# Reordering loads, stores and the first attention units in a fused attention and mixture-of-depths kernel

## The chip, the cores and the metric

The kernel runs on one core of one Trainium2 chip. The metric is the device time of one execution in microseconds; a smaller number is better. A core has five engines, each with its own stream of instructions in program order: TensorE (PE, matrix products and transposes; its weight loads are listed apart as PEld), VectorE (DVE), ScalarE (ACT), GpSimd (POOL) and SyncE (SP), which here only issues transfers. [...] In this kernel the schedule is written by hand: the order of the lines in the source is the order of each engine's instructions.

## The reference

Eight batches, eight heads, 576 positions, head dimension 64. Attention without a product of queries and keys: q is softmaxed over its head dimension, k over the positions, and `k^T v` (64 x 64 per head) is formed first. Then, for each batch, the 128 positions with the highest gate score go through an MLP (512 to 1024 to 512) and the others are passed through.

```python
def _attn_ref(q, k, v):
    q_s = np.exp(q - np.max(q, axis=-1, keepdims=True))
    q_s = q_s / (np.sum(q_s, axis=-1, keepdims=True) + 1e-09)
    k_s = np.exp(k - np.max(k, axis=2, keepdims=True))
    k_s = k_s / (np.sum(k_s, axis=2, keepdims=True) + 1e-09)
    kv = np.einsum('bhsd,bhse->bhde', k_s, v)
    return np.einsum('bhsd,bhde->bhse', q_s, kv)

def _moe_ref(x, w_gate, w1, w2, capacity):          # x: (8, 576, 512), the heads side by side
    scores = np.einsum('bsd,d->bs', x, w_gate)
    out = x.copy()
    for b in range(B):
        top_idx = np.argpartition(-scores[b], capacity)[:capacity]      # capacity 128
        xe = x[b, top_idx]
        ye = np.maximum(xe @ w1, 0.0) @ w2
        g = 1.0 / (1.0 + np.exp(-scores[b, top_idx]))
        out[b, top_idx] = x[b, top_idx] + g[:, None] * ye
    return out
```

## The kernel before

The work is cut into 16 units; a unit is four heads of one batch, so two units make one batch ("block"). All arithmetic is in fp32 but for the finding of indices. The steps of a unit u:

```python
LD = 3                                   # raw k, v, q: three buffers each, unit u uses u % 3
def load(u, which, queues=(nc.sync, nc.sync)):      # two transfers for each of k, v, q, issued by SyncE
    ...
def k_exp(u):   nc.scalar.activation(out=ke, in_=raw["k"][u % LD], func=AF.Exp)             # L217
def q_exp(u, i): nc.scalar.activation(out=st["qe", u][:, i], in_=qr[:, i], func=AF.Exp)     # L224, half i of q
def v_copy(u, engine=nc.vector):                                                           # L227
    engine.tensor_copy(out=v_ones[u % 2][:, :, :, :D], in_=raw["v"][u % LD])
def kv_mm(u):                            # L237: exp(k)^T [v, 1], 20 products
    ...
def kv_out(u):                           # DVE reciprocal L246, product with the gate weights wg L249,
    ...                                  # ACT copy to kv_w L250, DVE sum L251
def q_t(u, i, on_vector=False, wide=False):          # transposes of qe (L265 or L272), then scaled to qT
    ...                                              # on ACT (L278) or DVE (L276)
def x_mm(u, i, wide=False):              # L288 or L293: qT times kv_w, into PSUM tile "x" (two buffers)
    ...
def x_sums(u, i):   ...                  # DVE: 1 / sum (L309), gate scores (L310)
def x_scale(u, i):  ...                  # DVE: x times 1 / sum into xs (L315); xs has three buffers, one per block
def x_store(u):                          # L325: two transfers from xs to out, issued by SyncE
    ...
def kv_and_exp(u):
    kv_mm(u); q_exp(u, 0); kv_out(u); q_exp(u, 1)
def ready(u, engine=nc.vector):
    k_exp(u); v_copy(u, engine)
```

For a block b, `score` and `score_row` turn the gate scores into a row on all partitions (TensorE transposes L351, ScalarE copies L354 and L356), `compare` counts for each position how many others come before it (L364, five steps on VectorE), `hits` marks the chosen ones (L381), `find` collects their row numbers (TensorE L391), `fetch` gathers the rows back from `out` by an indirect transfer (L405, GpSimd), `turn` transposes them (L440), `mlp1` and `mlp2` are the two products of the MLP (L459, L469, eight pieces each), `finish` adds (L482) and `put` scatters the rows back (L474). Block 0 alone gets its rows by products with a one-hot matrix (`select`, L420) instead of a gather.

Units 0 to 2 are written out ahead of the loop, of which the parts touched are:

```python
    set_not_before(range(2))
    nc.vector.tensor_copy(out=wg..., in_=g_ps[:, :4 * D])
    ready(0)
    kv_mm(0)
    q_exp(0, 0)
    kv_out(0)
    q_exp(0, 1)
    load(3, "kvq")
    load_w2(0)
    ...                                   # units 0 and 1, load(4, "kvq"), load_w2(1), unit 2 up to its transposes
    for r in range(R):                    # R = 5
        compare(0, r)
        if r == N2 - 1:                   # N2 = 4
            x_mm(2, 0)
        for n in range(n_sl):             # n_sl = 1
            select(0, n, r)
    x_mm(2, 1)
    k_exp(3)
    x_out(2, 0)
    x_out(2, 1)
    v_copy(3)
    x_store(2)
```

The loop runs over s from 3 to 18. Stage s does the products of unit s (for s below 16) and half of the MLP of block (s - 3) // 2: `mlp1` in an odd stage, `mlp2` in an even one. The MLP's pieces are put between the other work to keep TensorE busy.

```python
    LAG = 3
    OWN = 3, 5, 7
    for s in range(LAG, NU + LAG):        # NU = 16
        ...
        own = s in OWN
        kv_next = s + 1 < NU and not own and s + 1 not in OWN
        ends = s // 2 if here and s % 2 == 1 else None              # the block that ends here
        chosen = (s - 2) // 2 if s % 2 == 0 and s <= NU else None   # the block whose rows are found here
        if own:
            if s > LAG:
                ready(s)
            pieces(2)
            kv_and_exp(s)
        if s == 6:
            load(8, "kvq")
        if s == 8:
            load(11, "kvq")
        if s == NU:
            each(fetch, 0)
        if here:
            q_t(s, 0)
            q_t(s, 1)
        if chosen is not None:
            each(hits, chosen)
        if kv_next:
            ready(s + 1)
        pieces(1) if own else pieces(2)
        if chosen is not None:
            each(find, chosen)
            each(fetch, chosen)
        if here:
            ...                           # x_mm, x_sums, (score), x_scale of unit s
            x_store(s)
        if s == 5:
            x_store(0)
            x_store(1)
        if kv_next:
            kv_and_exp(s + 1)
        if s < 6:
            load(s + 2, "kvq")
        elif s == 7:
            load(9, "kvq")
            load(10, "kvq")
        elif 8 <= s < NU - 4:
            load(s + 4, "kvq")
        pieces(1 if own or ends is None else 2)
        if own:
            v_copy(s + 1)
        if ends is not None:
            score_row(ends)
            if own:
                k_exp(s + 1)
            for r in range(R):
                compare(ends, r)
        if s == LAG + 1:
            for step in (hits, find, gate):
                each(step, 0)
        ...                               # gate of the chosen block
        pieces(1 if own else 3 if ends is None else 2)
        if own:
            kv_and_exp(s + 1)
        pieces(1)
        if second and mlp_b + 1 < B:
            each(turn, mlp_b + 1)
        pieces(KF - f_next)               # KF = 8
        ...                               # finish
```

In stages 3, 5 and 7 ("own") a unit's kv product is made in its own stage and the next unit's at the end of the same stage. In all other stages the kv product of the next unit is made after the x products.

Of the kernel before, what the change touches and what calls it, by code (L numbers as in the profile page):

```python
# [17 lines left out]
def kernel(  # L18
# [25 lines left out]
    N2 = R - 1  # L44
# [3 lines left out]
    KF = F // P  # L48
# [42 lines left out]
    NU = len(units)  # L91
# [116 lines left out]
    def set_not_before(rows):  # L208
        for r in rows:
            nc.vector.tensor_scalar(not_before[:, r], order_minus_p, float(r * P), TINY, op0=OP.is_ge, op1=OP.mult)  # L210
# [9 lines left out]
    def q_exp(u, i):  # L220
        if i == 0:
            st["qe", u] = at.tile([P, 2, R, 2, D], F32, tag="qe", name="qe")
        qr = raw["q"][u % LD].rearrange("p (i h) r d -> p i r h d", i=2)
        nc.scalar.activation(out=st["qe", u][:, i], in_=qr[:, i], func=AF.Exp)  # L224
# [16 lines left out]
    def kv_out(u):  # L241


        qd = units[u][1]
        kv = st.pop(("kv", u))
        nc.vector.reciprocal(out=krec[:, u], in_=kv[:, :, D])  # L246
        kw = kv_w[u % 2]
        prod = at.tile([P, 2, D], F32, tag="prod", name="prod")
        nc.vector.tensor_mul(prod, kv[:, :, :D], wg[:, qd])  # L249
        nc.scalar.copy(out=kw[:, :, :D + 1], in_=kv)  # L250
        nc.vector.reduce_sum(out=kw[:, :, D + 1], in_=prod, axis=AX.X)  # L251
# [3 lines left out]
    def q_t(u, i, on_vector=False, wide=False):  # L255

        if i == 0:
            st["qT", u] = at.tile([P, 2, R, 2, D], F32, tag="qT", name="qT")
        qe = st["qe", u] if i == 0 else st.pop(("qe", u))
        t_ps = ps.tile([P, 2, 512], F32, tag="x", name="x", bufs=2)  # L260
        if wide:
            to = st["qT", u][:, i].rearrange("p r a c -> p (r a c)")
            src = t_ps.rearrange("p a c -> p (a c)")[:, :R * P]
            for r in range(R):
                nc.tensor.transpose(out=src[:, r * P:(r + 1) * P], in_=qe[:, i, r].rearrange("p h d -> p (h d)"),  # L265
                                    identity=ident)
        else:
            to = st["qT", u][:, i].rearrange("p r a c -> p a r c")
            src = t_ps[:, :, :R * 64].rearrange("p a (r c) -> p a r c", r=R)
            for r in range(R):  # L270
                for a in range(2):
                    nc.tensor.transpose(out=t_ps[:, a, r * 64:(r + 1) * 64],  # L272
                                        in_=qe[part(a), i, r].rearrange("p h d -> p (h d)"),
                                        identity=ident[part(a), part(a)])
        if on_vector:
            nc.vector.tensor_scalar(to, src, krec[:, u, i:i + 1], None, op0=OP.mult)  # L276
        else:
            nc.scalar.activation(out=to, in_=src, func=AF.Copy, scale=krec[:, u, i:i + 1])  # L278
# [312 lines left out]
    def ready(u, engine=nc.vector):  # L591
        k_exp(u)
        v_copy(u, engine)
# [10 lines left out]
    for h in range(2):  # L604
        nc.tensor.matmul(out=g_ps[part(h), :4 * D], lhsT=ones_f,
                         rhs=w_row.rearrange("o (x h d) -> o h x d", h=2, d=D)[:, h], start=True, stop=True)
    set_not_before(range(2))
    nc.vector.tensor_copy(out=wg.rearrange("p a i d -> p (a i d)"), in_=g_ps[:, :4 * D])
    ready(0)
    kv_mm(0)  # L610
    q_exp(0, 0)
    kv_out(0)
    q_exp(0, 1)
    load(3, "kvq")
    load_w2(0)

# [32 lines left out]
    q_t(2, 0, wide=True)  # L649
    fill(4)  # L650
    q_t(2, 1, wide=True)
    for r in range(R):
        compare(0, r)
        if r == N2 - 1:
            x_mm(2, 0)
        for n in range(n_sl):
            select(0, n, r)
    x_mm(2, 1)
    k_exp(3)
    x_out(2, 0)  # L660
    x_out(2, 1)
    v_copy(3)
    x_store(2)

    LAG = 3
    OWN = 3, 5, 7
    number = good = None
    for s in range(LAG, NU + LAG):

        mlp_b, second = divmod(s - LAG, 2)  # L670
        piece = mlp2 if second else mlp1
        f_next = 0

        def pieces(n):
            nonlocal f_next
            for _ in range(n):
                each(piece, mlp_b, f_next)
                f_next += 1

        here = s < NU  # L680
        own = s in OWN
        kv_next = s + 1 < NU and not own and s + 1 not in OWN
        ends = s // 2 if here and s % 2 == 1 else None
        chosen = (s - 2) // 2 if s % 2 == 0 and s <= NU else None
        if own:
            if s > LAG:
                ready(s)
            pieces(2)
            kv_and_exp(s)
        if s == 6:  # L690
            load(8, "kvq")
        if s == 8:
            load(11, "kvq")
        if s == NU:
            each(fetch, 0)
        if here:
# [3 lines that stand above are left out]
            each(hits, chosen)  # L700
        if kv_next:
            ready(s + 1)
        if own:
            pieces(1)
        else:
            pieces(2)
        if chosen is not None:
            each(find, chosen)
            each(fetch, chosen)
        if here:  # L710
            x_mm(s, 0)
            x_mm(s, 1)
            x_sums(s, 0)
            x_sums(s, 1)
            if ends is not None:
                score(ends)
            x_scale(s, 0)
            x_scale(s, 1)
            x_store(s)
        if s == 5:  # L720
            x_store(0)
            x_store(1)
        if kv_next:
            kv_and_exp(s + 1)
        if s < 6:
            load(s + 2, "kvq")
        elif s == 7:
            load(9, "kvq")
            load(10, "kvq")
        elif 8 <= s < NU - 4:  # L730
            load(s + 4, "kvq")
        pieces(1 if own or ends is None else 2)
        if own:
            v_copy(s + 1)
        if ends is not None:
            score_row(ends)
            if own:
                k_exp(s + 1)
            for r in range(R):
                compare(ends, r)  # L740
        if s == LAG + 1:
            for step in (hits, find, gate):
                each(step, 0)
        if chosen is not None:
            each(gate, chosen)
        if good is not None and number is None:
            number = count_good(good)
        pieces(1 if own else 3 if ends is None else 2)
        if own:
            kv_and_exp(s + 1)  # L750
        pieces(1)
        if second and mlp_b + 1 < B:
            each(turn, mlp_b + 1)
        pieces(KF - f_next)
        if second:
            each(finish if mlp_b else finish_gated, mlp_b)
        if s == NU + 1:
            each(finish_rows, 0)
        if s == NU:
            good = in_range()  # L760
# [28 lines left out]
```

## Time and profile before

| | |
|---|---|
| time, median of 3 | 228.05 us (227.99 to 228.05) |
| span of the profiled execution | 228.4 us |
| transferred | 46.67 MB, mean 204 GB/s |
| busy: TensorE, VectorE, ScalarE, GpSimd | 204.3, 117.7, 86.6, 36.8 us |
| start of the loop (first MLP product) | 31.17 us |
| starts of s = 4, 5, 6, 7, 8, 9 | 46.87, 61.88, 77.49, 90.13, 105.59, 118.08 us |

The last two rows are read from the chain of work that ended last: the loop starts with the first group at L459, a later stage with the transposes of its unit (L272) or, where its kv product is its own, with the MLP pieces ahead of them. In the timelines a line holds start, length, engine, source line, operation, result and operands, shape and count, and in brackets how long the engine stood idle just before and what released it. The records count each fp32 product twice: unit products that the program issues 20 times are listed as x40.

### The profile page before, as it was taken

Reading aid. Unit: us, or ns where it says so; the run is one execution under the profiler, and the core shown is the slowest. Engines: PE = TensorE matmul, PEld = TensorE weight load, DVE = VectorE, ACT = ScalarE, POOL = GpSimd, SP = SyncE. Lnnn points to the kernel's source line nnn. Section 1 sums busy time; section 2 is a strip of 40 time slices with the busy share of each in tenths; the row PEclk is TensorE's granted clock in tenths of the full one; section 3 lists DMA queues with packets and bytes.
Section 4 is the critical chain, followed back from the end, with each engine's and each line's share of the span. In section 5 each row is a group of like instructions: output and inputs, shape, how many; then the busy total and the mean of one; then the engine's idle time right before and its main releaser. Section 6 shows DMA issues by size and latency. Waiting matters only on the chain.

```text
span 228.4 us, 7006 instructions
## 1 busy us (share of the span) xinstructions
PE 204.3 (89%) x2983; PEld 154.0 (67%) x2983; DVE 117.7 (52%) x353; ACT 86.6 (38%) x145; POOL 36.8 (16%) x93
## 2 busy tenths in 40 slices
PE   6789998896988988889999999999999999989970
PEld 2478797762577754777659965996599659747720
DVE  6477953937018651186635782568256824815010
ACT  3265444540275403455335452544354532201100
POOL 5024000311003010230113010401040103214101
PEclk9999999998899999999999999999999999999998
DMA  5999999573901999229999959468313131331101
GB/s 192 360 357 384 364 368 354 182 261 125 306 32 54 295 317 372 97 82 283 326 370 384 373 197 301 161 210 250 108 53 103 41 113 49 106 92 46 53 4 50
DMA packets 39305, 46.67 MB, mean 204 GB/s; under 512 B 2401, under 2 KB 36193, under 8 KB 39266
## 3 DMA queue, kind: packets, MB, share of 16 engines
q1 hardware_dynamic: 37712, 41.62, 54.5%
q0 software_dynamic: 1280, 4.20, 5.3%
q8 instruction: 25, 0.41, 0.7%
q10 hardware_dynamic: 274, 0.33, 0.4%
q14 instruction: 14, 0.11, 0.1%
HBM read 34.61 MB, written 11.53 MB: 202 GB/s over the span
## 4 chain that ended last, share of the span: by engine, by line
PE 64%; DVE 15%; DMA 9%; ACT 5%; issue 3%; POOL 1%; SPq 1%; POOLq 0%; ACTq 0%; DVEq 0%
PE mm L469 18%; PE mm L459 17%; PE x L293 9%; PE tp L237 8%; DVE junk L364 7%; DMA xr<-out_dram,idx 5%; PE x L272 4%; DMA q<-in_q_dram 4%; ACT qe L224 3%; DVE xs L315 3%; PE mm L420 2%; PE mm L440 1%; PE x L265 1%; PE x L288 1%; PE tp L351 1%
## 5 line engine op out<-in xcount | busy, mean ns | idle before, releaser
L459 PE MATMUL mm<-xT,w 128*128 128x128 f32 x512 | 64.2, 279 | 0.0
L459 PEld LDWEIGHTS mm<-xT,w 128*128 128x128 f32 x512 | 59.4, 192 | 3.7 <-ACT xT L447 1.9
L469 PE MATMUL mm<-w,hT 128*128 128x512 f32 x128 | 61.8, 618 | 0.0
L469 PEld LDWEIGHTS mm<-w,hT 128*128 128x128 f32 x128 | 23.0, 195 | 21.5 <-issue 20.7
L364 DVE SCALAR_TENSOR_TENSOR junk<-srow,s,not_before 128x576 bf16<-128x576 f32 x40 | 32.7, 817 | 7.8 <-ACT srow L356 6.8
L237 PE MATMUL tp<-v_ones,ke 128*64 128x65 f32 x640 | 23.3, 224 | 5.4 <-ACT ke L217 3.0
L237 PEld LDWEIGHTS tp<-v_ones,ke 128*64 128x64 f32 x640 | 20.7, 137 | 8.0 <-ACT ke L217 3.9
L224 ACT ACTIVATE qe<-q 128x640 f32<-128x640 f32 x32 | 23.5, 738 | 4.3 <-DMA q<-in_q_dram 2.5
L315 DVE TENSOR_TENSOR xs<-x,qrec 128x640 f32<-128x640 f32 x32 | 25.0, 816 | 0.0
L278 ACT ACTIVATE qT<-x,krec 128x640 f32<-128x640 f32 x30 | 22.5, 793 | 3.6 <-PE x L272 3.4
L293 PE MATMUL x<-kv_w,qT 64*64 64x66 f32 x1200 | 22.6, 221 | 1.1 <-issue 0.9
L482 DVE SCALAR_TENSOR_TENSOR o<-mm,g,xr 128x512 f32<-128x512 f32 x7 | 5.3, 751 | 34.6 <-PE mm L469 34.6
L293 PEld LDWEIGHTS x<-kv_w,qT 64*64 64x64 f32 x1200 | 19.8, 133 | 3.3 <-issue 1.6
L309 DVE RECIPROCAL qrec<-x 128x10 f32<-128x10 f32 x32 | 7.0, 220 | 28.4 <-PE x L293 28.2
L462 ACT ACTIVATE hT<-mm 128x512 f32<-128x512 f32 x16 | 9.5, 594 | 31.5 <-PE mm L459 31.5
L217 ACT ACTIVATE ke<-k 128x1280 f32<-128x1280 f32 x16 | 20.4, 1272 | 0.9 <-DMA k<-in_k_dram 0.9
L250 ACT COPY kv_w<-tp 128x130 f32<-128x130 f32 x16 | 4.3, 268 | 39.0 <-DVE prod L249 33.2
L405 POOL DMA_INDIRECT xr<-out_dram,idx x8 | 8.4, 1046 | 59.9 <-DVE sr L310 18.1
L447 ACT COPY xT<-mm 128x512 f32<-128x512 f32 x8 | 4.7, 585 | 34.2 <-PE mm L440 29.2
L474 POOL DMA_INDIRECT out_dram<-o,idx x7 | 8.3, 1182 | 55.1 <-DVE o L482 55.1
L272 PE MATMUL x<-ident,qe 64*128 64x64 f32 x260 | 12.2, 230 | 3.6 <-ACT qe L224 3.6
L272 PEld LDWEIGHTS x<-ident,qe 64*128 64x128 f32 x260 | 9.6, 139 | 8.4 <-ACT qe L224 4.4
(99 smaller groups left out, 146.6 us busy)
## 6 DMA issues: line engine op xcount, KB each, us to landing
v<-in_v_dram SPq DMA_DIRECT2D x16, 320.0 KB
q<-in_q_dram SPq DMA_DIRECT2D x16, 320.0 KB
out_dram<-xs SPq DMA_DIRECT2D x16, 320.0 KB
k<-in_k_dram SPq DMA_DIRECT2D x15, 320.0 KB
k<-in_k_dram SPq DMA_DIRECT2D x16, 256.0 KB
v<-in_v_dram SPq DMA_DIRECT2D x16, 256.0 KB
q<-in_q_dram SPq DMA_DIRECT2D x16, 256.0 KB
out_dram<-xs SPq DMA_DIRECT2D x16, 256.0 KB
```

The source lines that it names most:

```text
L217: nc.scalar.activation(out=ke, in_=raw["k"][u % LD], func=AF.Exp)
L224: nc.scalar.activation(out=st["qe", u][:, i], in_=qr[:, i], func=AF.Exp)
L237: nc.tensor.matmul(out=kv[part(h), i], lhsT=ke[:, 2 * i + h, r], rhs=vo[:, 2 * i + h, r], start=(r == 0), stop=(r == N2))
L272: nc.tensor.transpose(out=t_ps[:, a, r * 64:(r + 1) * 64], in_=qe[part(a), i, r].rearrange("p h d -> p (h d)"), identity=ident[part(a), pa ...
L278: nc.scalar.activation(out=to, in_=src, func=AF.Copy, scale=krec[:, u, i:i + 1])
L293: nc.tensor.matmul(out=x[part(c), h, r * C:(r + 1) * C], lhsT=qT[part(h), i, r, c], rhs=kv_w[u % 2][part(h), i], start=True, stop=True)
L315: nc.vector.tensor_mul(xs[b][:, :, qd, i].rearrange("p r h d -> p h r d"), x[:, :, :, :D], rec.to_broadcast([P, 2, R, D]))
L364: nc.vector.scalar_tensor_tensor(junk, st["srow", b], st["s", b][:, r:r + 1], not_before[:, r], op0=OP.subtract, op1=OP.is_ge, accum_out=s ...
L405: nc.gpsimd.indirect_dma_start(out=xr[:m], out_offset=None, in_=out_rows[:(place(b) + 1) * S], in_offset=bass.IndirectOffsetOnAxis(ap=st[" ...
L459: nc.tensor.matmul(out=h_ps[:, f % 4 * m:(f % 4 + 1) * m], lhsT=w1[:, d, f * P:(f + 1) * P], rhs=xT[:, d, :m], start=(d == 0), stop=(d == ...
L462: nc.scalar.activation(out=hT[:, f - 3:f + 1, :m], in_=h_ps[:, :4 * m].rearrange("p (f c) -> p f c", f=4), func=AF.Relu)
L469: nc.tensor.matmul(out=st["y", b, n][:m], lhsT=st["hT", b, n][:, f, :m], rhs=w2[:, f], start=(f == 0), stop=(f == KF - 1))
```

## The change

Only the order of instructions is changed. It has four parts.

- Unit 0: v's copy goes ahead of the copy of wg on VectorE, and both exps of q ahead of kv_out, which has a copy on ScalarE.
- Unit 3: its exps, v's copy and its kv product move from stage 3 to the stretch ahead of the loop. The first x product of unit 2 moves two rows earlier. With this, unit 4's kv product comes in the usual place of stage 3, after unit 3's x products.
- Of the stages with a kv product of their own only s = 5 remains, and both exps of q go ahead of that product. Unit 6's exp and copy move forward accordingly, and unit 7 is treated as any later one.
- Loads: k and v of unit 5 are issued before the loop and so before the store of unit 3; after stage s the load is always that of unit s + 3; in stage 5 unit 8's load goes ahead of the late stores of units 0 and 1.

In stage 4 the steps of block 0 (hits, find, gate), which serve only to scatter its rows later, are spread over the stage. The next block's rows are turned always one piece before the last of the MLP.

```diff
     set_not_before(range(2))
+    ready(0)
     nc.vector.tensor_copy(out=wg..., in_=g_ps[:, :4 * D])
-    ready(0)
     kv_mm(0)
     q_exp(0, 0)
+    q_exp(0, 1)
     kv_out(0)
-    q_exp(0, 1)
     ...
     q_t(2, 1, wide=True)
+    k_exp(3)
     for r in range(R):
         compare(0, r)
-        if r == N2 - 1:
+        if r == 1:
             x_mm(2, 0)
         for n in range(n_sl):
             select(0, n, r)
     x_mm(2, 1)
-    k_exp(3)
+    q_exp(3, 0)
+    q_exp(3, 1)
+    v_copy(3)
     x_out(2, 0)
+    kv_mm(3)
     x_out(2, 1)
-    v_copy(3)
+    kv_out(3)
     x_store(2)
+    load(5, "kv")
     ...
-    OWN = 3, 5, 7
+    OWN = 5
     ...
-        kv_next = s + 1 < NU and not own and s + 1 not in OWN
+        kv_next = s + 1 < NU and s + 1 != OWN
+        first_hits = s == LAG + 1
-        if own:
-            if s > LAG:
-                ready(s)
+        if s == LAG:
             pieces(2)
-            kv_and_exp(s)
-        if s == 6:
-            load(8, "kvq")
-        if s == 8:
-            load(11, "kvq")
+        if s == OWN:
+            ready(s)
+            q_exp(s, 0)
+            q_exp(s, 1)
+            pieces(2)
+            kv_mm(s)
+            kv_out(s)
     ...                                  # q_t of unit s, hits of the chosen block, ready(s + 1) if kv_next
-        if own:
-            pieces(1)
-        else:
-            pieces(2)
+        if first_hits:
+            each(hits, 0)
+        pieces(1 if s in (LAG, OWN) else 2)
     ...                                  # find, fetch; x_mm, x_sums, x_scale, x_store of unit s
-        if s == 5:
+        if s == LAG:
+            load(5, "q")
+            load(6, "kvq")
+        elif s < NU - 3:
+            load(s + 3, "kvq")
+        if s == OWN:
             x_store(0)
             x_store(1)
         if kv_next:
             kv_and_exp(s + 1)
-        if s < 6:
-            load(s + 2, "kvq")
-        elif s == 7:
-            load(9, "kvq")
-            load(10, "kvq")
-        elif 8 <= s < NU - 4:
-            load(s + 4, "kvq")
-        pieces(1 if own or ends is None else 2)
-        if own:
-            v_copy(s + 1)
+        if first_hits:
+            each(find, 0)
+        pieces(1 if ends is None else 2)
         if ends is not None:
             score_row(ends)
-            if own:
-                k_exp(s + 1)
             for r in range(R):
                 compare(ends, r)
-        if s == LAG + 1:
-            for step in (hits, find, gate):
-                each(step, 0)
+        if first_hits:
+            each(gate, 0)
     ...                                  # gate of the chosen block
-        pieces(1 if own else 3 if ends is None else 2)
-        if own:
-            kv_and_exp(s + 1)
-        pieces(1)
+        pieces(KF - 1 - f_next)
         if second and mlp_b + 1 < B:
             each(turn, mlp_b + 1)
-        pieces(KF - f_next)
+        pieces(1)
```

## The prediction

> **What bounds the kernel now.** I read the page's slices first, then a table of stages, then the TensorE timeline. The page's rows (each digit a fortieth of the span, 5.71 us):
>
> ```profile
> PE 204.3 (89%) x2983; PEld 154.0 (67%) x2983; DVE 117.7 (52%) x353; ACT 86.6 (38%) x145; POOL 36.8 (16%) x93
> ...
> PE   6789998896988988889999999999999999989970
> ...
> PEclk9999999998899999999999999999999999999998
> DMA  5999999573901999229999959468313131331101
> ```
>
> TensorE is the bound: 89% busy, no other engine over 52%, and a 64% share of the chain. From about slice 20 on it is full; in slices 5 to 19 it has gaps, and in slices 10 and 11 its clock dips. The DMA is full in slices 2 to 7 (354 to 384 GB/s), so an early gain can also run into arrivals.
>
> Next, the stages of the main loop (columns: window, length, busy and count of PE, PEld, DVE, ACT, POOL, clock, DMA share, GB/s). The first six rows are s = 3 to 8, the last two are s = 11 and 12, two undisturbed stages of the same kinds:
>
> ```profile
> 31.17:46.87 15.70, 13.57 (x257) 12.57 (x251) 10.31 (x29) 7.29 (x13) 1.80 (x7) 1.00 0.86 290
> 46.87:61.88 15.01, 12.68 (x131) 6.50 (x131) 5.72 (x19) 3.39 (x8) 1.19 (x1) 0.89 0.68 215
> 61.88:77.49 15.61, 13.54 (x252) 12.50 (x251) 8.45 (x25) 8.01 (x14) 1.79 (x7) 1.00 0.34 114
> 77.49:90.13 12.64, 10.80 (x127) 5.81 (x126) 3.67 (x12) 3.39 (x8) 1.01 (x1) 1.00 1.02 332
> 90.13:105.59 15.46, 13.46 (x250) 12.50 (x249) 9.93 (x27) 7.24 (x13) 3.13 (x8) 1.00 0.45 145
> 105.59:118.08 12.49, 11.88 (x166) 7.02 (x165) 4.96 (x17) 6.00 (x11) 1.02 (x1) 1.00 1.01 335
> 141.45:152.94 11.49, 11.49 (x211) 11.05 (x213) 7.15 (x19) 5.25 (x9) 2.65 (x8) 1.00 0.57 185
> 152.94:164.54 11.60, 11.47 (x168) 6.84 (x169) 6.45 (x20) 5.37 (x9) 1.03 (x1) 1.00 0.66 211
> ```
>
> The reader is to see that the last two rows hold almost no TensorE idle time, while s = 3, 5 and 7 take 15.5 to 15.7 us instead of 11.49. One kv product of that, 1.32 us, is extra work (those stages hold two); the rest, nearly 3 us each, is waiting. What is waited for stands in the brackets of the TensorE timeline (start, length, operation, count, idle before it and releaser):
>
> ```profile
> 9.56 1.39 PE L237 MATMUL tp<-v_ones,ke 128*64 128x65 f32 x40 [1.36 <-ACT qe L224]
> ...
> 36.19 0.53 PE L272 MATMUL x<-ident,qe 64*128 64x64 f32 x10 [1.00 <-ACT qe L224]
> ...
> 42.67 1.39 PE L237 MATMUL tp<-v_ones,ke 128*64 128x65 f32 x40 [1.01 <-ACT ke L217]
> ...
> 55.23 0.28 PE L391 MATMUL tp<-vals,hit 128*128 128x5 bf16 x5 [1.66 <-DVE hit L381]
> ```
>
> The second and third recur with 0.99 to 1.01 us at 66.82 and 73.29 (s = 5) and at 94.92 and 101.40 (s = 7).
>
> [...] around the 1.66 us wait at 55.23 its busy time is 0.77 of 2 us in 54 to 56, and the granted clock is 0.86, 0.50 and 0.79 in 54:56, 56:58 and 58:60. [...] the trace shows qe's second half at 66.03, behind kv_w's copy (65.86), which waited for VectorE. [...] SyncE's waits here show stores on DVE's xs for 46.4 us in total. [...] The gather of s = 6 took 7.30 us beside loads, the one at 201.66 took 3.27.
>
> **The change part by part.** No TensorE work is added or removed; only waits can go or come.
>
> Start. v's copy goes ahead of wg's, which waits for the small product that ends at 8.21 (7.51 + 0.70). The copy (0.82, now 8.60 to 9.42) can end by about 8.3, and the kv product starts there instead of at 9.56: 1.25 us. Both exps of q now stand ahead of kv_w's copy, so qT(0, 0) starts near 10.4 instead of 12.23. What follows soon meets arrivals: v's second unit was waited for until 12.20 on GpSimd, then the copy takes 1.25, so kv product 1 cannot start before 13.5 (now 15.90); unit 2's cannot before 17.25 + 1.25 = 18.5 (now 20.45). I take 1.9 us saved at the row's comparison and hence at the loop's start.
>
> Unit 3 ahead of the MLP. Its kv product adds 1.33 before the loop and leaves s = 3. From the GB/s row, k, v and q of unit 3 land near 25.5, 27 and 29 us; the product needs them at about 29.7, so I put no wait there. The loop starts at 31.17 - 1.9 + 1.33 = 30.6.
>
> Stages 3 to 8, from the undisturbed 11.49 (odd) and 11.60 (even):
> - s = 3: one kv product, no inner waits, the MLP in one more burst: 11.49 + 0.2 = 11.7 (was 15.70).
> - s = 4: no kv product: 11.60 - 1.33 = 10.3; find of block 0 adds 0.3. One MLP piece (about 1 us) fewer stands between the score row and find, and in the undisturbed stage hits end at 132.1, just as find is reached: 0.9 wait. Small issue gaps 0.3. The gather of block 1 falls among the loads of units 5, 6 and 7; with 7.3 us instead of 3.3 it lands up to 1.9 us after TensorE wants it: 1.2. Sum 13.0 (was 15.01). The 1.66 wait and the half clock (0.14 x 2 + 0.50 x 2 + 0.21 x 2 = 1.7 us lost) go, because block 0's hits are made next to block 1's and its find follows the x product.
> - s = 5, still its own: two kv products, 11.49 + 1.33; exps of q before the product end near the product's end (k's exp 1.27, two exps about 1.4), so only 0.2 for one more burst and 0.2 for k's exp of unit 6: 13.2 (was 15.61).
> - s = 6: 11.60 + 0.9 (find again, one piece fewer) + 0.3 = 12.8; it now holds unit 7's kv product (was 12.64 without).
> - s = 7: 11.5 (was 15.46). s = 8: 11.60 + 0.3 = 11.9 (was 12.49).
>
> Sum: 11.7 + 13.0 + 13.2 + 12.8 + 11.5 + 11.9 = 74.1, so s = 9 starts at 30.6 + 74.1 = 104.7 instead of 118.08. The order from s = 9 on is the same but for loads three units ahead instead of four. A load issued after s's store still has over 1.5 stages, about 17 us, until its k is used, and three arrays of 0.59 MB at 370 GB/s take 4.8. So the rest stays 228.40 - 118.08 = 110.3: span 215.0, and 214.7 by the median, which is 0.35 under the profiled span. My list takes each wait that I found and none that I didn't; I add 1.3 for those: **216.0 us**.
>
> **Rivals.**
> 1. Arrivals take the gain. For it: DMA is full to about 40 us, and unit 4's k, v, q land near 33, 35 and 36.5 while the new order asks for them from 34.5 on; v's copy stands in VectorE's FIFO ahead of unit 3's sums, so a late v holds the x buffers. Against it: in my schedule these miss by under 0.6 us. If each early arrival costs, the start's 1.9 us and another 1.5 go: about 219.5.
> 2. The gather becomes the wait. Loads that used to sit behind stores run early, so block 1's gather shares the engines with up to three units' loads. For it: 7.30 against 3.27 us. If it lands 3 us late, TensorE may also fall to half clock as at 55 us: 3 + 1.7 less the 1.2 counted, so 219.5.
> 3. The stores of units 0 and 1 now go behind unit 8's load. They free the buffer that s = 6's xs writes; by my count they land near 74 us, where VectorE wants it at 72.5. That holds VectorE 1.5 us beside 7 us of TensorE work, so nothing; if the backlog is 8 us longer it costs about 2 to 3 us.
> 4. Everything fits and no arrival shows: without the 1.3 and the 1.2, 213.5.
>
> **Range and chances.** The waits removed are read from the trace, 12 to 13 us with the start, and none of the rivals gives back more than 4 alone. Two together reach 222. So 212.8 to 220.5, faster by over 2% (under 223.5) 0.93, within 2% 0.05, slower 0.02.
>
> **What would show it.** Right: the first kv product near 8.3; the loop's first MLP product near 30.6; no bracket from qe or ke of about 1 us in s = 3, 5, 7; clock 1.00 throughout 45 to 60; s = 9 starting near 105; a small bracket from hit before find in s = 4 and 6; the tail as long as before. Wrong: TensorE idle from DMA (v, k or xr) of over 2 us, a dip of the clock in the loop, VectorE waiting for out_dram stores near s = 6, or the loads of s over 9 arriving late.

## The result and the profile after

The changed kernel took 216.76 us (median of 4, 215.09 to 218.49) against 228.05 us: a ratio of 0.948, 95% interval 0.9426 to 0.9535. The ratios here and below are of the mean times of undisturbed executions (the record counts the 218.49 as disturbed, in a state of lower clock, 0.985 instead of 0.994 to 0.995), the medians of all. The profiled execution spans 214.7 us instead of 228.4; as a whole that execution took 216.52 us, and the profiled one of the kernel before 230.25, which is 2.2 over its median. Differences between the two traces are therefore larger than those between the times: 13.7 us of span against 11.3. The page's rows for it:

```profile
PE 197.9 (92%) x2980; PEld 151.2 (70%) x2983; DVE 118.9 (55%) x353; ACT 87.4 (41%) x145; POOL 35.4 (16%) x93
...
PE   5998998889999899999979999999999999899970
...
PEclk9999999999999999999999999999999999999997
DMA  5999999997937999494949387586930412311101
```

TensorE's busy time fell by 6.4 us, though it does the same work: 1.7 us of that is, by the prediction's estimate, the half clock that is gone from slices 10 and 11 (before, the granted clock was 0.50 from 55.45 to 58.86; now it is 1.00 in all six stages below). Of the rest a part lies in the x products (L293): one takes 221 ns in both kernels, but the time covered by all 1200 records fell from 22.6 to 21.2 us, so they overlap more. The other 7.3 us are idle time. The DMA is now full up to slice 9 instead of 7.

The stages, s = 3 to 8 and the rest (columns as before: window, length, busy and count of PE, PEld, DVE, ACT and POOL, clock, DMA share, GB/s):

```profile
31.46:45.05 13.59, 12.00 (x215) 11.29 (x211) 6.37 (x20) 5.92 (x11) 1.33 (x7) 1.00 1.07 376
45.05:55.76 10.71, 10.13 (x132) 5.59 (x131) 7.84 (x25) 2.89 (x6) 1.19 (x1) 1.00 0.91 303
55.76:69.15 13.39, 13.12 (x252) 12.35 (x253) 6.27 (x19) 8.65 (x14) 1.33 (x7) 1.00 0.63 196
69.15:81.11 11.96, 11.38 (x167) 6.66 (x169) 7.33 (x22) 5.38 (x9) 1.02 (x1) 1.00 0.99 323
81.11:93.11 12.00, 11.77 (x212) 11.19 (x213) 7.18 (x19) 5.38 (x9) 2.66 (x8) 1.00 0.73 239
93.11:104.38 11.27, 11.27 (x167) 6.79 (x169) 6.43 (x20) 5.37 (x9) 1.03 (x1) 1.00 0.71 222
104.38:214.70 110.32, 100.73 (x1397) 76.58 (x1397) 53.58 (x154) 37.30 (x64) 19.64 (x41) 0.99 0.45 144
```

The six stages take 72.9 us instead of 86.9, 1.33 of which moved ahead of the loop; the rest of the program takes 110.3 as before. The idle times on TensorE that remain (start, length, operation, count, idle before and releaser):

```profile
8.28 1.39 PE L237 MATMUL tp<-v_ones,ke 128*64 128x65 f32 x40 [0.17 <-DVE v_ones L227]
...
37.28 0.65 PE L237 MATMUL tp<-v_ones,ke 128*64 128x65 f32 x15 [0.58 <-DVE qrec L309]
38.94 0.92 PE L237 MATMUL tp<-v_ones,ke 128*64 128x65 f32 x25 [1.01 <-issue]
...
48.33 0.28 PE L391 MATMUL tp<-vals,hit 128*128 128x5 bf16 x5 [0.58 <-DVE hit L381]
...
62.55 1.39 PE L237 MATMUL tp<-v_ones,ke 128*64 128x65 f32 x40 [0.19 <-ACT ke L217]
...
72.40 0.28 PE L391 MATMUL tp<-vals,hit 128*128 128x5 bf16 x5 [0.57 <-DVE hit L381]
...
111.19 2.05 PE L459 MATMUL mm<-xT,w 128*128 128x128 f32 x16 [1.42 <-issue]
```

The brackets of about 1 us from qe and ke are gone. Two kinds are new. One is a wait at 37.28 for VectorE's copy of unit 4's v:

```profile
36.31 0.83 DVE L227 COPY v_ones<-v 128x1280 f32<-128x1280 f32 x1 [4.04 <-DMA v<-in_v_dram]
```

The copy ended at 37.14 and the product starts 0.14 us later, as unit 0's does after its copy; the bracket names the reciprocal that VectorE did next, which the product does not read. The other kind are gaps put down to "issue", in the middle of a product or ahead of one, of which more below.

### The profile page after: what moved, and what is told of

Its sections match the earlier page's. It is cut to its first block, busy times and chain, and to the rows that moved or that the text cites. A ratio compares the mean times of both kernels' runs of the same rounds, so it can differ in the third digit from the quotient of the medians.

```text
span 214.7 us, 7006 instructions
## 1 busy us (share of the span) xinstructions
PE 197.9 (92%) x2980; PEld 151.2 (70%) x2983; DVE 118.9 (55%) x353; ACT 87.4 (41%) x145; POOL 35.4 (16%) x93
## 4 chain that ended last, share of the span: by engine, by line
PE 64%; DMA 14%; DVE 12%; ACT 3%; issue 3%; POOL 1%; POOLq 0%; ACTq 0%; DVEq 0%
PE mm L469 22%; PE mm L459 20%; DMA v<-in_v_dram 8%; PE x L293 7%; PE tp L237 7%; DVE junk L364 6%; DMA q<-in_q_dram 4%; PE x L272 3%; DMA xr<-out_dram,idx 2%; PE mm L440 2%; PE tp L351 1%; DVE hit L381 1%; DVE not_before L210 1%; ACT srow L354 1%; ACT qT L278 1%
## 5 line engine op out<-in xcount | busy, mean ns | idle before, releaser
L459 PE MATMUL mm<-xT,w 128*128 128x128 f32 x512 | 63.0, 278 | 1.4 <-issue 1.4
L469 PE MATMUL mm<-w,hT 128*128 128x512 f32 x128 | 59.9, 603 | 0.0
L469 PEld LDWEIGHTS mm<-w,hT 128*128 128x128 f32 x128 | 22.6, 190 | 20.8 <-issue 19.9
L237 PE MATMUL tp<-v_ones,ke 128*64 128x65 f32 x640 | 22.7, 224 | 2.9 <-issue 1.2
L237 PEld LDWEIGHTS tp<-v_ones,ke 128*64 128x64 f32 x640 | 20.2, 137 | 4.9 <-issue 2.1
L293 PE MATMUL x<-kv_w,qT 64*64 64x66 f32 x1200 | 21.2, 221 | 0.1
L293 PEld LDWEIGHTS x<-kv_w,qT 64*64 64x64 f32 x1200 | 19.0, 134 | 1.8 <-ACT qT L278 0.6
L227 DVE COPY v_ones<-v 128x1280 f32<-128x1280 f32 x14 | 11.5, 821 | 5.6 <-DMA v<-in_v_dram 5.6
L272 PEld LDWEIGHTS x<-ident,qe 64*128 64x128 f32 x260 | 9.1, 139 | 4.7 <-ACT xT L447 3.8
```

The source lines that it names most:

```text
L237: nc.tensor.matmul(out=kv[part(h), i], lhsT=ke[:, 2 * i + h, r], rhs=vo[:, 2 * i + h, r], start=(r == 0), stop=(r == N2))
L272: nc.tensor.transpose(out=t_ps[:, a, r * 64:(r + 1) * 64], in_=qe[part(a), i, r].rearrange("p h d -> p (h d)"), identity=ident[part(a), pa ...
L293: nc.tensor.matmul(out=x[part(c), h, r * C:(r + 1) * C], lhsT=qT[part(h), i, r, c], rhs=kv_w[u % 2][part(h), i], start=True, stop=True)
L459: nc.tensor.matmul(out=h_ps[:, f % 4 * m:(f % 4 + 1) * m], lhsT=w1[:, d, f * P:(f + 1) * P], rhs=xT[:, d, :m], start=(d == 0), stop=(d == ...
L469: nc.tensor.matmul(out=st["y", b, n][:m], lhsT=st["hT", b, n][:, f, :m], rhs=w2[:, f], start=(f == 0), stop=(f == KF - 1))
```

## The experiments

The kernel before took 228.0 to 230.7 us on the chips that were used, so each version is judged by its ratio to the kernel before on its own chip; 0.01 is 2.3 us. Some versions ran on one chip and can also be set against each other: the new start, all but the move, the old start and the old steps; both versions of the loads, the 72 instructions, and w2 late; the changed kernel once more and the two versions with the MLP ahead. "Old" below means the order of the kernel before.

| version | median us | ratio and interval |
|---|---|---|
| before, new start only | 226.86 | 0.9937 (0.9901 to 0.9972) |
| before, new loads only | 229.18 | 0.9937 (0.9911 to 0.9963) |
| before, all but the move of the units | 221.74 | 0.9763 (0.9644 to 0.9882) |
| changed | 216.76 | 0.948 (0.9426 to 0.9535) |
| changed, once more | 219.26 | 0.9537 (0.9487 to 0.9587) |
| changed, old start | 216.75 | 0.9533 (0.9443 to 0.9624) |
| changed, old steps of block 0 | 218.62 | 0.9601 (0.948 to 0.9721) |
| changed, old loads | 223.73 | 0.970 (0.9651 to 0.975) |
| changed, 72 more instructions at the start | 217.20 | 0.9415 (0.9369 to 0.946) |
| changed, w2 late and score row early | 218.71 | 0.9446 (0.9386 to 0.9506) |
| changed, MLP ahead of the kv product | 219.35 | 0.9549 (0.9501 to 0.9596) |
| the last two together | 218.61 | 0.951 (0.9465 to 0.9555) |
| changed, masks early | 217.52 | 0.9554 (0.9506 to 0.9603) |

### The start alone

The edit swaps `ready(0)` with the copy of wg, and `kv_out(0)` with `q_exp(0, 1)`, in the kernel before; nothing else.

> The kernel before with only the new start of unit 0 (v's copy ahead of wg's, both exps of q ahead of kv_out). In this kernel nothing early in the loop waits for arrivals (v of unit 4 is copied only after 41 us), so the prediction's step, 1.9 us saved at the start, should come through: about 226.2 us. Rival: arrivals hold units 1 and 2, so that no more than 0.5 us is left: 227.5 or more.

Measured: 0.9937, that is 1.4 us of 228.05. The interval, 0.6 to 2.3 us, takes in the 1.9 and leaves out the rival's 0.5. In its trace the loop starts at 30.00 instead of 31.17 (1.17 us).

### The changed kernel with the old start

> The changed kernel with the old start of unit 0. If the start is worth its 1.9 us in the changed kernel too, about 218.7 us. What the trace after suggests instead: the loop's start moved by 1.0 us only (31.17 + 1.33 against 31.46), and in stage 3 v of unit 4, which lands at 36.3 whatever the start does, holds VectorE and through it TensorE (0.58 and perhaps the 1.01 after it). Then a later start uses up that wait: 217.0 to 217.6 us, and the wait before the kv product of unit 4 shrinks or goes.

Measured: 0.9533, which cannot be told from the changed kernel (0.948 and 0.9537). The trace says what the times cannot. Two lines of its TensorE timeline:

```profile
32.29 2.05 PE L459 MATMUL mm<-xT,w 128*128 128x128 f32 x16
...
39.68 0.92 PE L237 MATMUL tp<-v_ones,ke 128*64 128x65 f32 x25 [1.41 <-issue]
```

The loop starts 0.83 us later than in the changed kernel, and the wait for v of unit 4 is gone, as expected: the product starts at 37.60 instead of 37.28, only 0.32 later. But the gap inside the product grew from 1.01 to 1.41, so its second part is 0.74 later, and the transposes of s = 9 start at 105.31 instead of 104.31. So the start is worth about 1 us up to there: the wait for v did use up most of it, and the gap gave it back. The spans are the same (214.5 and 214.7) because this trace lacks the gap of 1.42 us at 111.19.

### Block 0's steps put back together

```diff
-        if first_hits:
-            each(hits, 0)
...
-        if first_hits:
-            each(find, 0)
...
         if first_hits:
-            each(gate, 0)
+            for step in (hits, find, gate):
+                each(step, 0)
```

> The changed kernel with hits, find and gate of block 0 put back together after the compares of stage 4. By the prediction the wait of 1.66 us before find returns, and with it the half clock near 50 to 56 us (1.7 us lost): about 220.1 us, with a granted clock below 1 in that stretch. Rival: only the wait returns and the clock holds: about 218.4. Second rival: the wait is hidden by other work: 216.8.

Measured: 218.62, 0.9601. TensorE waits 1.85 us for hits at 52.54, and then (columns: window, length, TensorE busy and count, clock, DMA share, GB/s):

```profile
50.00:52.00 2.00, 0.69 (x2) 1.00 0.87 284
52.00:54.00 2.00, 1.46 (x8) 0.83 0.55 192
54.00:56.00 2.00, 2.00 (x4) 0.50 0.99 292
56.00:58.00 2.00, 2.00 (x5) 0.82 1.00 334
```

Stage 4 takes 14.5 us instead of 10.7. In this trace wait and half clock came back together, as the prediction had it. The times do not settle what it costs: the median of four executions (217.28 to 220.16) lies 1.9 us over that of the version with the old start on the same chip, near the first rival's 218.4, but the intervals of the two overlap.

The half clock need not come with the wait: the kernel before with the new loads, below, has the same wait of 1.66 us and no half clock in its trace. The eight records of the MLP behind it take 3.68 us there and 5.38 here. What decides is not shown; this is what the traces hold. In the kernel before the granted clock changed at 7.66, 55.45, 58.86 and 226.11, the last three 14, 15 and 64 steps of 3.41 us after the first; in the changed kernel it changed at 7.36 and 212.16, 60 steps apart. In the step that ended when the clock fell, TensorE was busy for 51% of the time in the kernel before and for 46% here. With the new loads an instant at this spacing, 53.19, falls into the wait (52.66 to 54.32), and the steps on its two sides are 70% and 67% busy. The author's reading is that it matters where the wait lies between the instants. No run tests this, and the busy share does not decide alone: with only the new start one step of 49% (112.46 to 115.87) was followed by no fall.

### All but the move of the units

The kernel before with the new start, the new loads and the spread steps of block 0, but `OWN = 3, 5, 7` as before.

> The kernel before with the new start, the new order of loads and stores and the spread steps of block 0, but with units 3, 5 and 7 still making their kv products in their own stages. If the move of the units is the largest part (two waits of 1.0 us in each of s = 3, 5, 7 and their short bursts, 2.2 to 2.9 us a stage), about 223 us. Rival: the new order of loads and stores is what brings the gain, and this kernel comes near 217.5.

Measured: 221.74, 0.9763, which makes 222.6 on a chip where the kernel before takes 228.05. Its TensorE timeline keeps both waits in each of the three stages; those of s = 3 and the first of s = 5:

```profile
35.59 0.52 PE L272 MATMUL x<-ident,qe 64*128 64x64 f32 x10 [1.00 <-ACT qe L224]
...
42.06 1.39 PE L237 MATMUL tp<-v_ones,ke 128*64 128x65 f32 x40 [1.01 <-ACT ke L217]
...
61.53 0.53 PE L272 MATMUL x<-ident,qe 64*128 64x64 f32 x10 [0.99 <-ACT qe L224]
```

On the same chip the changed kernel with the old start has 0.9533: 5.2 us, close to half of the whole gain, and the two intervals do not overlap. (That version lacks the new start, so the move is worth at least this, if the start costs nothing.) The trace also shows that the steps of block 0, spread, leave no wait for hits in s = 4 without the move. Undone one at a time from the changed kernel, no part costs more than the move, though the loads, next, come near.

### The loads alone, and the changed kernel without them

In the first, the kernel before gets `load(5, "kv")` after `x_store(2)` and, after each stage's store, `load(s + 3)` (in stage 3 the rest of unit 5 as well). In the second, the changed kernel gets the old list of loads.

> The kernel before with only the new order of loads and stores. By the sum of the prediction the loads bring nothing themselves, as TensorE waited for ScalarE and VectorE and not for arrivals: within 1.5 us of the kernel before, and what there is comes from the gathers of s = 6 and 8, which no longer share the engines with two units' loads. Rival: the loads are the main part of the change, and 5 us or more come from them.

Measured: 0.9937, 1.4 us. In its trace the gather of s = 6 costs TensorE 0.35 us instead of 1.05, and the wait of 1.66 us for hits is followed by no half clock (mean granted clock 0.995 against 0.988). By the reading above, the clock may be a matter of where the wait fell and not of the loads; no run separates the two.

> The changed kernel with the old order of loads and stores. If that order only makes room for the move of unit 7, then here k and v of unit 7, which are issued behind three stores at about 70 us and land near 77, hold ScalarE and VectorE in stage 6, where they are wanted at 71: TensorE waits 4 us or more and the time is 221 us or more. Rival: the new order is worth nothing, and this kernel is within 1 us of the changed one.

Measured: 223.73, 0.970, so 3.7 to 5.0 us are lost against the changed kernel's 0.9537 and 0.948 (both on other chips). VectorE, stage 6:

```profile
76.24 0.83 DVE L227 COPY v_ones<-v 128x1280 f32<-128x1280 f32 x1 [3.89 <-DMA v<-in_v_dram]
```

and TensorE:

```profile
77.22 2.44 PE L237 MATMUL tp<-v_ones,ke 128*64 128x65 f32 x40 [3.20 <-DVE no L395]
79.58 6.27 PE L469 MATMUL mm<-w,hT 128*128 128x512 f32 x10
```

VectorE comes to unit 7's copy at 72.3 and waits until 76.2; TensorE waits 3.2 us, not the 4 expected, and is slower after it: the product takes 2.44 instead of 1.39, the MLP pieces 6.27 instead of 4.56, and the mean granted clock of the execution is 0.976 instead of 0.994. A second loss stands in stage 8, where TensorE waits 1.68 us for the gather at 110.86. So the loads bring little in the old order of units, and the new order of units, with the rest of the change, loses 35 to 42% of the gain without them; the other 6.8 us (0.970) do not need them.

### Gaps that nothing releases

The trace after and those of the first two versions of the changed kernel had TensorE idle after 15 of 40 records of unit 4's kv product. The warm-up was changed to move the instruction stream:

```diff
-    for n in range(WARM):
-        nc.tensor.matmul(out=w_ps, lhsT=ones_b[:, :P], rhs=ones_b, start=True, stop=True)
+    for n in range(4 * WARM):
+        c = slice(n % 4 * P, (n % 4 + 1) * P)
+        nc.tensor.matmul(out=w_ps[:, c], lhsT=ones_b[:, :P], rhs=ones_b[:, c], start=True, stop=True)
```

> The changed kernel with the twelve warm-up products of 512 columns cut into 48 of 128 columns, which adds 72 instructions to TensorE's stream at the start and no time. Three traces show TensorE idle in the middle of unit 4's kv product (after 15 of 40 records, for 1.0 to 1.4 us, with nothing that it waits for), about 1.3 us after a 16 KB packet of the instruction queue ends. If the fetch of the next block of instructions is the cause, that gap leaves this product and comes 72 instructions earlier in the program, in unit 3's x products, or goes where TensorE waits anyhow; the time may move by 1 us either way. If it is something that belongs to this product (its PSUM bank, its operands), the gap stays after 15 records.

Measured: 217.20, 0.9415. The gap left the kv product:

```profile
38.05 0.57 PE L294 MATMUL x<-kv_w,qT 64*64 64x66 f32 x20 [1.06 <-issue]
```

It now comes before the last 20 of 80 records of unit 3's x products. Each record is a weight load and a product; from there to the old place are 20 + 15 records, 70 instructions, and 72 were added. So the gap belongs to a place in the stream of instructions and not to the work. The trace of the changed kernel has 25 packets of 16,384 B in the instruction queue. By the record of packets one ends at 37.51 us in the changed kernel, and the gap that opens at 37.93 ends at 38.94, 1.4 us after it; in this version a packet ends at 36.42 and the gap 1.6 us later. Two later gaps of the changed kernel, those that end at 86.56 and 111.19, also end 1.4 and 1.5 us after such a packet. The three begin after 595, 1358 and 1739 records of TensorE, which are 763 and 381 apart: within one record, the first distance is twice the second. So the author puts these gaps down to the wait for such a packet; the first one lies where 240 instructions of small products (80 records of x and 40 of kv) follow each other in 2.7 us. How a packet is called, and which engine it is for, is not shown.

Not all gaps without a releaser are of this kind. In stage 6 TensorE stood idle for 0.39 us after 5 of 40 records of the kv product, both in this version (75.03) and in the second trace of the changed kernel (74.93), though the stream had moved by 72 instructions, and in the changed kernel's trace the last such packet had ended 9.7 us before. Their cause is open. Whether the ratio of 0.9415 is a gain over the changed kernel is open, as the two did not run on one chip.

### Taking the waits for v and hits away

```diff
-    load_w2(0)          # after load(3, "kvq")
     ...
     load(4, "kvq")
+    load_w2(0)
     load_w2(1)
     ...
-        pieces(1 if ends is None else 2)
+        pieces(1 if ends is None or s <= OWN else 2)
```

> The changed kernel with both halves of w2 loaded behind unit 4 and, in stages 3 and 5, the score row one MLP piece earlier. v of unit 4 should land 2.8 us earlier (1.05 MB at 370 GB/s), so the wait of 0.58 us in stage 3 goes, and compares and hits end about 1 us earlier, so both waits of 0.58 us before find go: 1.7 us less than the changed kernel, 215.0 us. If the waits were only the cover of something else (the instruction gap, the gather), less than 0.5 us is gained.

Measured: 218.71 (216.73 to 220.81), 0.9446. In its trace the waits for v and for hits are gone, but the gap inside unit 4's product is there still and is longer: 2.79 us, and behind it the granted clock is 0.61 in 40:42 and 0.54 in 42:44. That execution was the longest of six, so the length is not set against other traces. The changed kernel did not run on this chip, so no gain can be read from the times.

### The MLP pieces between the x products and the kv product

The changed kernel once more, for comparison on the same chip:

> The changed kernel itself once more, on the chip of the next two, so that they can be set against it: a ratio of 0.95 to the kernel before, and in the trace the gap without a releaser inside unit 4's kv product, after 15 of 40 records, of 1 us or more.

Measured: 0.9537; its trace has a wait for v of 1.09 us and the gap after 15 records with 0.46 us. The expectation of 1 us or more missed; together the two are 1.55, and 1.59 in the first trace of the changed kernel, and the product's second part starts at 38.93 and 38.94. In both traces the packet of instructions ended at 37.51. So in stage 3 the gap after this packet seems to have set the time, and the wait for v lay under it.

```diff
+        if ends is not None:
+            pieces(2)
         if kv_next:
             kv_and_exp(s + 1)
     ...
-        pieces(1 if ends is None else 2)
+        if ends is None:
+            pieces(1)
```

> The changed kernel with the two MLP pieces of the odd stages put between unit s's x products and unit s + 1's kv product instead of behind it. [...] the 2 us of MLP in between give the fetch its time: the gap of 1.0 us in stage 3 goes, those of 0.2 to 1.4 us in stages 7 and 9 too, and the time falls by 1 to 2 us against the changed kernel. If the fetch is not the cause, the gap stays after 15 records of the product and the time stays.

Measured: 219.35, 0.9549, no gain. The gap of stage 3 left the product, but the idle time did not all go:

```profile
36.72 2.05 PE L459 MATMUL mm<-xT,w 128*128 128x128 f32 x16
39.19 1.39 PE L237 MATMUL tp<-v_ones,ke 128*64 128x65 f32 x40 [0.41 <-ACT qe L224]
```

The product runs its 40 records in one piece; stages 7 and 9 have no such gap either. But the 0.41 ahead of it is no wait for qe, which this product does not read: its ke was ready at 36.81 and its copy of v ended at 37.60. It comes after 596 records of TensorE, where the changed kernel's gap comes after 595, and ends 1.6 us after a packet that ended at 37.60. So it is in all likelihood the same gap at the same place in the stream, which now holds the end of the MLP pieces; TensorE arrived there later, so less is left of it. What was won came back as this and as other waits: 0.23 in each score row for kv_w, and 0.8 instead of 0.6 for hits.

> The same with both halves of w2 behind unit 4 and the score rows of stages 3 and 5 one piece earlier. The version of this that kept the pieces behind the kv product lost the waits for v and for hits, but its gap in the kv product grew from 1.0 to 2.8 us and took the clock to half. With one piece in between (1 us) a part of that gap should be left, 0.5 to 1.8 us; the time is 0.5 to 2 us under the changed kernel. If the gap only fills up whatever wait is taken away, the time is that of the changed kernel within 0.5 us.

Measured: 218.61 (218.20 to 219.09) against 219.26 on the same chip. The medians differ by 0.65 us, within the lower part of what was expected, but the intervals (0.9465 to 0.9555, 0.9487 to 0.9587) overlap: not settled. In its trace no gap and no wait for v is left in stage 3 (v's copy begins at 33.98 instead of 36.77, the 2.8 us that were estimated), but now TensorE waits 1.33 us for the gather of stage 4. No version was shown to beat the changed kernel on one chip.

### What became of the start

On VectorE the answer for the masks' line in the changed kernel gives the shortest, median and longest of five (ns):

```profile
L210 DVE TENSOR_SCALAR not_before<-order_minus_p x5: 447/449/1503, 5.7 to 13.7; 128x576 bf16<-128x576 f32 x5
```

and in the kernel before:

```profile
L210 DVE TENSOR_SCALAR not_before<-order_minus_p x5: 449/452/454, 5.7 to 14.7; 128x576 bf16<-128x576 f32 x5
```

One mask took 1.05 us more, while GpSimd copied v of unit 1 (12.26 to 13.51). It is the second of the three, from 12.32 to 13.83, stretched by about what was left of a copy of 1.25 us. With only the new start, and in the second trace of the changed kernel, the three masks take 2.24 us together beside that copy; with the old start the copy ends at 13.79, the masks begin at 13.86, and they take 1.19. So a mask is long where it runs beside the copy; why is not shown. The last version moves the masks away:

```diff
-    set_not_before(range(2))
+    set_not_before(range(4))
     ...
-    set_not_before(range(2, R))
     ...
     kv_out(1)
+    set_not_before(range(4, R))
```

> The changed kernel with two of the three late not_before masks made ahead of v's copy, where VectorE is idle, and the third behind kv_out of unit 1. In the traces with the new start one of these masks took 1.50 us instead of 0.45 because GpSimd copied v of unit 1 at the same time, and x's sums of unit 0 began late. If that is what ate the start's gain, the sums of unit 0 begin about 1.2 us earlier (near 12.9 instead of 14.1), the loop starts 0.5 to 1.0 us earlier (30.5 to 31.0 instead of 31.5), and, as v of unit 4 still lands near 36.3, TensorE's wait for it grows by as much: no gain at the end, within 0.7 us of the changed kernel. If the arrivals of units 1 and 2 hold the start instead, the loop starts at 31.4 to 31.6 all the same.

Measured: 217.52, 0.9554. The sums of unit 0 begin at 12.52 instead of 14.11 and unit 1's x products at 16.51 instead of 17.69, but:

```profile
19.46 1.39 PE L237 MATMUL tp<-v_ones,ke 128*64 128x65 f32 x40 [1.18 <-POOL v_ones L227]
```

Unit 2's kv product waits for GpSimd's copy of v, which begins at 18.15 (18.39 in the changed kernel), and the loop starts at 31.23. The first product here began at 8.10 instead of 8.28, so 0.05 of those 0.23 us are left to explain. The masks were a real hold-up but not the one that counts: v of unit 2 is. Why does its copy begin at 18.2 to 18.4 us and not at 17.25 as in the kernel before? The transfer is issued at the same time, and by the record of landings 15 of its 16 shares are in by 17.02 (all 16 by 17.05 in the kernel before); the last one lands at 18.19. A packet of 16,384 B of the instruction queue ran from 15.35 to 16.50, 1.15 us, about by what that share is late. In the kernel before, and in the changed kernel with the old start, this packet runs only from 17.48 and 17.29, and the copy begins at 17.25 and 17.55. So the earlier start seems to bring this packet forward, ahead of a part of v, and so to delay the copy that it needs next. This is the author's reading of the traces alone, and the packet does not decide by itself: with 72 more instructions such a packet ran from 15.64, and all of v was in by 17.39. No run moved this packet by itself.

## Why the prediction was right

216.0 us was foretold and 216.76 measured. The mechanism held: the waits of s = 3, 5 and 7 went with the move of the units, and this is the largest part. But part of the agreement is errors that cancel. Against the sum (times in us; the loop's start and then the lengths of the stages, with the bounds of the table of stages):

| | predicted | measured |
|---|---|---|
| loop starts | 30.6 | 31.46 |
| s = 3 | 11.7 | 13.6 |
| s = 4 | 13.0 | 10.7 |
| s = 5 | 13.2 | 13.4 |
| s = 6 | 12.8 | 12.0 |
| s = 7 | 11.5 | 12.0 |
| s = 8 | 11.9 | 11.3 |
| s = 9 starts | 104.7 | 104.4 |
| the rest | 110.3 | 110.3 |

- The start was mis-sized: 1.9 us were taken to the loop, 1.04 came (31.17 + 1.33 - 31.46). The first kv product did start near 8.3 (8.28). The bound on unit 2 was put at 18.5 from the kernel before's 17.25 + 1.25, but GpSimd's copy moved to 18.39 and the product to 19.70. The masks, stretched by 1.05 us, were not thought of either.
- "Nearly 3 us each, is waiting" was read too high: TensorE was idle for 2.0 to 2.1 us in each of s = 3, 5 and 7 (15.70 less 13.57 in s = 3). The rest of the difference was counted as busy, in shorter runs of products (ten of the transposes at L272 take 0.53 us in the kernel before, twenty in one run 0.84 after). The sum compared whole stages, so it was right all the same.
- The move of units 3 and 7 and the exps of s = 5 did what was said: no bracket of 1 us from qe or ke is left, s = 5 is right to 0.2 us, and the 0.19 for unit 6's k was foretold as 0.2. Without the move of the units 5.2 us are lost.
- "k, v and q of unit 4 land near 33, 35 and 36.5 ... these miss by under 0.6 us" was nearly so: v's copy began at 36.31, and TensorE waited 0.58 (1.09 in the second trace). The gap after the packet of instructions, 1.01, was not thought of. Together they are 1.59 of the 1.9 us by which s = 3 is too short in the sum.
- s = 4 was put 2.3 us too long: its products took 10.13 us where 10.6 had been put, the wait before find was 0.58 and not 0.9, and the gather was not late at all, where 1.2 had been put. It was issued at 50.02 and TensorE took its rows at 54.38 without a wait; the longest gather took 5.5 us, not 7.3. Rival 2 did not happen in the changed kernel. It did in the version that asked for the rows earlier (1.33).
- The half clock went, as said, and came back with the wait (block 0's steps put back). It is less certain than the prediction made it, since one trace had the wait without it; the kernel before may owe it to where the wait fell.
- Rival 1 happened in part (unit 4's and unit 2's v), with about 1.5 us in all; unit 3's v was late as well, copied from 28.63 after a wait and not there near 27, but no TensorE wait came of it; rival 3 did not: VectorE shows no wait for the late stores in stage 6.
- The 1.3 us added for waits not found was luck. The sum without it, a span of 215.0, was already within 0.3 us of the measured 214.7, in which the gaps after such packets, 1.01, 0.23 and 1.42 (2.66 in all), are made up for by stages that were put too long. It was the step from span to time that was wrong: 0.35 was taken off, but the profiled execution of the kernel before was 2.2 us over its median, and a span of 214.7 goes with a time of 216.52, 1.8 more. So this step was 2.2 us off, and the 1.3 made up for more than half of it.
- The rest is 110.3 in both by chance: the gap of 1.42 at 111.19 is mostly made up by stages 10, 12 and 14, which take 11.22 us instead of 11.6. In the second trace of the changed kernel they take 11.6 again, with gaps of 0.39 in the kv product of stages 6 and 8, so this is not the change.

## What to carry to other kernels

Where the bound engine works from a fixed order, find two stages of the same kind, one with and one without the trouble, and price the change by their difference and the brackets in between; this gave the size here. A new order of computing can need its loads in a new order: the loads alone gave 1.4 us, the rest without them 6.8, and both together 10.6 to 11.9. When one wait is taken away, look for what it covered: three times here something stood right behind it, behind the wait for v the gap after a packet of instructions, then the gather, and behind the masks the arrival of v.

## What had not been expected of the hardware

- In runs of small products TensorE stood idle for 0.2 to 1.4 us with nothing that released it, until 1.4 to 1.6 us after a packet of 16,384 B of instructions had ended. The one such gap that was tested kept its place in the stream when the work was moved against it.
- One of the sixteen shares of a load landed at 18.19 us and the other fifteen by 17.02; such a packet, 1.15 us long, had ended at 16.50. That it held the share up is the author's reading.
- A mask on VectorE took 1.50 us instead of 0.45 beside a GpSimd copy of 1.25 us.
- The same wait of 1.66 us on TensorE was followed by 3.41 us of half clock in one kernel and by none in another. In the two traces before and after, the clock changed only at instants a whole number of 3.41 us apart; in the kernel with the new loads such an instant cut the wait in two, and whether that decided is not shown.
